# Value product on 64x64 tiles, one matmul per head; attention weights copied once; in-weight rows in their own order; tokens by groups; a new written opening

## The chip, the cores and the metric

The kernel runs on one core of one Trainium2 chip. The metric is the device time of one execution in microseconds. Before the change, three runs gave 1189.91 to 1191.05 us with a median of 1190.45 us. All durations below come from one further execution, taken with the hardware profiler.

Names of the engines: PE is TensorE (matmuls), PEld its weight loads, DVE is VectorE, ACT is ScalarE, POOL is GpSimd, SP is SyncE, which issues the DMAs here.

## The reference, cut to what matters

Chunked attention with a few memory keys, then two feed-forward layers. Four batches, 8 heads, 768 positions, head size 64; chunks of 32 queries see 8 memory keys, 16 positions to the left, their own 32 and 8 to the right, 64 keys in all.

```python
for c in range(nc):                       # 24 chunks of 32 queries, per batch and head
    k_full = np.concatenate([mem_k, k_ctx], axis=2)   # up to 64 keys
    v_full = np.concatenate([mem_v, v_ctx], axis=2)
    scores = scale * np.matmul(q_c, k_full.transpose(0, 1, 3, 2))
    a = np.exp(scores - np.max(scores, axis=-1, keepdims=True))
    a = a / (np.sum(a, axis=-1, keepdims=True) + 1e-09)
    out[:, :, c_start:c_end] = np.matmul(a, v_full)
x = out.transpose(0, 2, 1, 3).reshape(3072, 512)
h = x @ w_in;  x = (h * sigmoid(1.702 * h)) @ w_out              # 512 -> 2048 -> 512
g = x @ w_gate;  y = (silu(g) * (x @ w_val)) @ w_out2            # 512 -> 1536 -> 512
```

## The kernel before, in words

**Tiling.** The 3072 tokens are 6 blocks of 512 tokens; a block is 4 groups of 128 tokens, a group 4 chunks of 32. One group is one attention job over all 8 heads, so there are 24 groups. Each goes through: scores on TensorE (`scores_first` for the first eight groups, `scores` for the rest), maximum and subtraction on VectorE (`exponents`), exponential on ScalarE, sums and normalisation on VectorE (`st_sums`, `st_weigh`), a transposition of the weights on TensorE into PSUM (`turn`, L158), copies of the transposed weights into SBUF on ScalarE (`keep_e`, L167), the value product on TensorE (`values`, L174), a copy of its output into x (`keep_x`, L188), and a store of x (`store_x`, L193).

**The value product.** Head pair `a`, chunk `c`: the 128 rows of the transposed weights hold the 64 keys of the even head above the 64 keys of the odd head. `keep_e` writes them as a block diagonal (`ebd`, even head in the upper rows and one half of the columns, odd head in the lower rows and the other half); its other blocks are cleared once (`zero`). The product contracts over all 128 rows, with the 64 value columns as the loaded operand and 64 columns of `ebd` as the streamed one. The output of head pairs `a` and `a + 1` goes to the upper and the lower 64 partitions. So the rows of x stand in another order than the reference's, and the rows of the in-weights are brought into that order when they are loaded: two DMAs of 256 KB for each in-weight tile, each onto 64 partitions, in runs of 128 numbers of 8 bytes (`load_raw`, L281). Other weight tiles take one DMA of 512 KB (L276).

**Weights.** They arrive as 8-byte numbers and are turned into fp32 words by ScalarE and VectorE (`take_words`, `shift_words`, `join_words`), then split into a high and a low part (`split_hi` on ScalarE, `split_lo` on GpSimd). Matmuls take three passes over high and low parts.

**Feed-forward.** A unit is one column block of a layer, computed with seven half-size products (a Strassen scheme): `Tokens` makes the sums of quarters of x, `unit` (and the letters `qa` to `qg` of the opening) the products, L450; `down` accumulates the output products, L585. The first block's first units are plain products, `plain_up`, L546.

**What sets the order.** PE, ACT, DVE and POOL run in the order in which the program is written. For the first part that order is a table of step names, `OPENING`, in which SP's loads stand too: `ldq`, `ldk`, `ldv`, `ldw` load q, k, v and a weight tile, `sc` is a group's scores, `te` its transposition, `ec` the copies, `pv` the value product, `hi`, `xf`, `xl` the parts of x, `ua` and `ub` a plain product. The number behind a name is the group or the tile. Groups 0 to 11 are in the table. Groups 12 to 23 are worked off between the parts of later units by `attention`, `run` and `PLACES`. Behind the opening a scheduler places SP's DMAs.

Of the kernel before, what the change touches and what calls it, by code (L numbers as in the profile page):

```python
# [57 lines left out]
def tile_attention_moe_moe(  # L58
# [11 lines left out]
    def pool(name, bufs, space=None):  # L70
# [89 lines left out]

    def weights_at(g):
        return ebd[g % 2 if g < 2 * GRP else 0]

    def keep_e(g, ps, engs):
        for e, copy in enumerate(engs):
            r = slice(64 * e, 64 * e + 64)
            copy(weights_at(g)[r, :, :, e, :], ps[r].rearrange("p a (c q) -> p a c q", c=4))  # L167

    def values(g, ps, v):
        ps = ps.rearrange("p (a q) -> p a q", a=KC)  # L170
        for a in range(0, HP, 2):
            for c in range(4):
                for j in range(2):
                    nc.tensor.matmul(  # L174
                        ps[64 * j : 64 * j + 64, a : a + 2, CH * c : CH * c + CH],
                        v[:, a + j, c, :],
                        weights_at(g)[:, a + j, c].rearrange("p e q -> p (e q)"),
                        start=True,
                        stop=True,
                    )  # L180
        return ps

    def keep_x(g, ps):
        b, i = divmod(g, GRP)
        if b not in xf:
            xf[b] = xpool.tile([P, KC, BLK], F32, tag="xf", name="xf")
        dst = xf[b][:, :, i * P : i * P + P]
        nc.scalar.copy(dst, ps)  # L188
        xq[g] = dst

    def store_x(g):
        b, i = divmod(g, GRP)
        nc.sync.dma_start(out=xd[b][:, :, i * P : i * P + P], in_=xq[g])  # L193

# [18 lines left out]
    def st_et(g):  # L213
        keep_e(g, turn(bank("ps_t"), et.pop(g)), (nc.scalar.copy,) * 2)

# [174 lines left out]
    class Tokens:  # L390


        def __init__(self, src, engs, apart=False):
            n = BLK // 2
            self.apart = apart
            self.b11, self.b12 = src[:, 0:2, :n], src[:, 0:2, n:]
            self.b21, self.b22 = src[:, 2:4, :n], src[:, 2:4, n:]
            self.engs = engs
            self.ops = [None] * 7

        def sum(self, k):
# [40 lines left out]

# [395 lines left out]
    def tokens():  # L838
        if not tok:
            tok.append(Tokens(xf[1], [G, G, G, V, G, V, V, V, G, V, V], True))  # L840
        return tok[0]
# [78 lines left out]
    OPENING = """  # L920
        z0 tb0 z1 ldk0 ldq0 ldq1 ldw0 ldq2 ldk1 ldk2 ldk3 sc0 ldv0 ldq3 mx0 ldq4 ex0 ldw1 pr0 sm0 cs0 sc1 ldv1
        ra0 ct0 ldv2 rc0 wa0 sc2 mx1 z2 ldq5 wg0 ex1 ldq6 wal0 te0 sm1 ldq7 mx2 ra1 sc3 ldk4 ec0 rc1 wg1 ex2 sm2
        pr1 ldw2 te1 mx3 ra2 pv0 ldk5 ec1 rc2 cs1 ldk6 ex3 ct1 ldk7 pv1 hi0 wg2 sumA0 ldv3 wv0 sm3 wb0 xf0 wbl0
        te2 ra3 ldw3 hiA0 sumB0 rc3 sc4 wg3 ec2 te3 mx4 wvl0 hiB0 pv2 loA0 ldw4 pr2 ldw5 ex4 cs2 loB0 sc5 ldv4
        xf2 sm4 xf1 ct2 xl0 st0 ra4 hi2 rc4 wg4 wa1 ldw6 ec3 wal1 sc6 mx5 ldw7 hi1 xl2 mx6 pv3 ex5 te4 ldk8 xl1
        sm5 ex6 sc7 hi3 sm6 ldq8 pr3 xl3 ra6 ra5 ldv5 pr4 cs3 ec4 rc5 ua0 ct3 ldv6 mx7 ldq9 sumA1 wb1 ua1 wv1
        pr5 st1 rc6 ex7 wg5 sumB1 ub0 hiA1 wg6 st2 xf3 loA1 ub1 cs4 hiB1 sm7 th0 ct4 wvl1 te5 st3 ra7 th1 ua2
        loB1 ldw8 gt0 ec5 rc7 gt1 wbl1 ub2 gc0 wg7 pr6 rs0 ldw9 gc1 cs5 pv5 th2 rs1 pr7 gt2 sc8 wo0 ct5 gc2 wol0
        pv4 ldk9 xf5 rs2 wo1 mx8 te7 ldv7 xf4 wol1 ldq10 te6 ec7 st4 cs6 ua3 st5 ct6 ex8 cs7 pr8 dn0 sm8 wo2 ct7
        ra8 wol2 ub3 ec6 rc8 ldw10 wg8 wo3 pv6 cs8 th3 wol3 ct8 dn1 pr9 ldv8 gt3 ldw11 wa2 pv7 cs9 wal2 gc3 ct9  # L930
        xf6 sc9 xf7 ldv9 rs3 sumA2 tc0 st7 ts0 te8 ldq11 tc1 dm1 ldk10 ts2 ts1 ec8 mx9 st6 dn2 tl0 tc3 ev1 pr10
        pv8 tl3 tc2 sy1 sumB2 ex9 qa0 ts3 ldv10 tc5 dm0 tl1 cs10 cp0 sm9 tc4 qc0 tl5 tl2 ev0 qb0 cu0 ct10 sy0
        tc6 qe0 tl4 ab0 ra9 qd0 pr11 tl6 wv2 sc10 rc9 cm0 wvl2 wg9 xf8 qf0 ldk11 ac0 hiA2 te9 ad0 hiB2 loA2 qg0
        st8 mx10 ka0 ldq12 dn3 ma0 loB2 kb0 ex10 dm2 mb0 kc0 ldw12 sm10 mc0 dm3 md0 ldw13 ra10 ec9 rc10 sc11 kd0
        ev2 wg10 pv9 wo4 ldk12 ev3 wol4 te10 cs11 xf9 ldv11 ya0 mx11 ec10 st9 sy3 sy2 yb0 ct11 ex11 sm11 wo5
        pv10 pr12 wol5 ldw14 ra11 yc0 pr13 rc11 ldv12 wg11 xf10 cs12 te11 st10 ct12 yd0 ec11 cs13 ldw15 ct13 wa3
        pv11 wv3 sumA3 qa1 xf11 ldv13 st11 qb1 cp1 wvl3 hiA3 qc1 sumB3 pr14 ab1 qd1 cu1 qe1 wal3 cm1 hiB3 qf1
        ac1 loB3 qg1 ad1 pr15 cs14 ka1 qa2 cs15 loA3 ldw16 ma1 kb1 qb2 cp2 mb1 kc1 qc2 ab2 mc1 qd2 kd1 cu2 md1
        qe2 cm2 ct14 qf2 ya1 ac2 wo6 ldw17 ad2 wol6 ct15 ka2 qg2 kb2 wo7 ldw18 yb1 ma2 wol7 kc2 yc1
    """  # L940
# [58 lines left out]
    for n, (ph, b, ua, ub) in enumerate(seq):  # L999
# [6 lines left out]
        for u in range(ua, ub):  # L1006
# [101 lines left out]
```

## Time and profile before

| | |
|---|---|
| median of three runs | 1190.45 us |
| the profiled execution: its own time | 1190.33 us |
| the profiled execution: span from first to last instruction | 1188.6 us |
| mean granted TensorE clock over the span | 0.991 |
| busy: PE, PEld | 1151.3 us (97%), 1039.6 us (87%) |
| busy: DVE, ACT, POOL | 652.1 (55%), 568.1 (48%), 354.9 us (30%) |
| chain that ended last, by engine | PE 86%, DMA 5%, DVE 3%, ACT 2%, issue 2%, POOL 1% |
| moved by DMA | 131.47 MB in 62920 packets, 26208 of them under 2 KB |

The busy share of TensorE is a mean over stages with different limits, so it is read by stage. Busy time of PE is the union of its records, and a matmul's end is modelled, so records overlap: what a group of matmuls costs is read from the distance between starts rather than from the mean length of one record.

### The profile page before, as it was taken

What the parts mean: (1) busy time and instruction counts of PE and PEld (TensorE: products, weight loads), DVE (VectorE), ACT (ScalarE), POOL (GpSimd) and SP (SyncE); (2) the same over time, 40 slices, a digit from 0 to 9 for tenths busy, and PEclk for the clock granted to TensorE, in tenths of its full rate; (3) what the DMA queues carried; (4) which work ended last, traced back from release to release, by engine and by line L of the source; (5) the groups of instructions that cost most, each with busy time, mean ns of one, the idle gap of its engine ahead of it and who ended that gap; (6) DMA issues with size and microseconds to landing.
All of it is one profiled execution on the core that took longest, in us unless ns stands there. A gap on an engine that the chain in (4) does not pass through costs nothing.

```text
span 1188.6 us, 22301 instructions
## 1 busy us (share of the span) xinstructions
PE 1151.3 (97%) x8908; PEld 1039.6 (87%) x8908; DVE 652.1 (55%) x1117; ACT 568.1 (48%) x1185; POOL 354.9 (30%) x321
## 2 busy tenths in 40 slices
PE   4889999999999999999999999999999999999998
PEld 3778888888989999999988989999999999999997
DVE  5886756565765444443466564453556554453553
ACT  4866555455565454444455544343445544243342
POOL 4564221202454232321235433021345521021010
PEclk9889999999999999999999999999999999999999
DMA  9977354441454313322333321210225130320302
GB/s 304 296 253 231 110 157 120 130 140 63 137 166 118 106 66 114 131 74 62 106 116 107 106 99 36 72 71 1 89 89 178 36 103 5 107 92 15 107 25 83
DMA packets 62920, 131.47 MB, mean 111 GB/s; under 512 B 5728, under 2 KB 26208, under 8 KB 60512
## 3 DMA queue, kind: packets, MB, share of 16 engines
q1 hardware_dynamic: 62816, 130.05, 34.9%
q8 instruction: 70, 1.15, 0.4%
q14 instruction: 34, 0.28, 0.1%
HBM read 98.57 MB, written 31.46 MB: 109 GB/s over the span
## 4 chain that ended last, share of the span: by engine, by line
PE 86%; DMA 5%; DVE 3%; ACT 2%; issue 2%; POOL 1%; SPq 0%; DVEq 0%; ACTq 0%; POOLq 0%
PE y L585 35%; PE ps_a L450 27%; PE ps_c L450 12%; PE ps_b L450 9%; DMA raw<-in_wr 2%; PE ps_s L201 1%; PE ps_o L174 1%; DMA q<-in_qg 1%; DMA w<-in_kg 1%; DMA xd<-xf 1%; PE ps_t L158 1%; PE ps_v L174 1%; ACT ebd L167 0%; PE ps_u L546 0%; ACT g L551 0%
## 5 line engine op out<-in xcount | busy, mean ns | idle before, releaser
L450 PEld LDWEIGHTS ps_a<-b,w 128*128 128x128 f32 x2832 | 384.3, 189 | 39.6 <-DVE ps_a L502 4.2
L450 PE MATMUL ps_a<-b,w 128*128 128x256 f32 x2832 | 397.5, 283 | 5.7 <-DVE ps_a L502 2.1
L585 PE MATMUL y<-gs,w 128*128 128x512 f32 x1152 | 298.6, 395 | 0.6 <-DVE gs L565 0.5
L585 PE MATMUL y<-w,gs 128*128 128x512 f32 x864 | 247.7, 395 | 0.6 <-DVE gs L565 0.5
L585 PEld LDWEIGHTS y<-gs,w 128*128 128x128 f32 x1152 | 204.2, 189 | 36.2 <-DVE gs L565 1.4
L450 PE MATMUL ps_c<-b,w 128*128 128x256 f32 x1224 | 179.1, 282 | 0.0
L450 PEld LDWEIGHTS ps_c<-b,w 128*128 128x128 f32 x1224 | 167.1, 190 | 8.8
L585 PEld LDWEIGHTS y<-w,gs 128*128 128x128 f32 x864 | 144.2, 190 | 14.4 <-DVE gs L565 1.7
L258 POOL TENSOR_TENSOR w<-wf,w 128x512 fp32r<-128x512 f32 (+1 forms) x68 | 78.3, 1152 | 222.0 <-ACT w L255 221.9
L450 PE MATMUL ps_b<-b,w 128*128 128x256 f32 x900 | 135.5, 287 | 1.7 <-DVE ps_b L821 1.2
L450 PEld LDWEIGHTS ps_b<-b,w 128*128 128x128 f32 x900 | 120.4, 193 | 5.9 <-issue 1.7
L553 ACT ACTIVATE g<-ps_b 128x512 f32<-128x512 f32 x72 | 43.1, 598 | 166.1 <-DVE ps_b L508 166.1
L436 DVE TENSOR_TENSOR b<-xl,b 128x512 fp32r<-128x512 f32 x72 | 64.3, 893 | 80.4 <-ACT b L432 80.3
L502 DVE TENSOR_TENSOR ps_a<-m,ps_a 128x256 f32<-128x256 f32 x115 | 48.9, 426 | 104.0 <-PE ps_a L450 98.0
L492 ACT COPY u<-ps_a 128x256 f32<-128x256 f32 x115 | 43.0, 373 | 107.8 <-PE ps_a L450 107.6
L415 POOL TENSOR_TENSOR xl<-xl,t 128x512 f32<-128x512 f32 x18 | 23.3, 1296 | 231.3 <-DVE t L412 230.0
L565 DVE TENSOR_TENSOR gs<-ps_a,gs 128x512 fp32r<-128x512 f32 x118 | 80.8, 685 | 10.2 <-ACT gs L561 9.8
L487 DVE TENSOR_TENSOR ps_b<-p,ps_b 128x256 f32<-128x256 f32 x115 | 49.2, 427 | 61.3 <-PE ps_b L450 54.0
L561 ACT CAST gs<-ps_a 128x512 fp32r<-128x512 f32 x118 | 69.8, 592 | 22.5 <-DVE ps_a L531 15.6
L531 DVE TENSOR_TENSOR ps_a<-g,ps_a 128x512 f32<-128x512 f32 x72 | 50.0, 694 | 45.7 <-PE ps_a L450 45.2
L483 ACT COPY p<-ps_a 128x256 f32<-128x256 f32 x115 | 43.0, 374 | 60.3 <-PE ps_a L450 56.4
L508 DVE TENSOR_TENSOR ps_b<-u,ps_c 128x256 f32<-128x256 f32 x102 | 43.5, 426 | 50.1 <-PE ps_c L450 49.8
(123 smaller groups left out, 1190.6 us busy)
## 6 DMA issues: line engine op xcount, KB each, us to landing
raw<-in_wr SPq DMA_DIRECT2D x49, 512.0 KB, 3.4
xl<-yd SPq DMA_DIRECT2D x12, 1024.0 KB, 4.8
vm<-in_vg SPq DMA_DIRECT2D x22, 512.0 KB, 6.0
kbd<-in_kg SPq DMA_DIRECT2D x32, 256.0 KB, 4.2
raw<-in_wr SPq DMA_DIRECT2D x30, 256.0 KB, 5.3
yp<-o SPq DMA_DIRECT2D x24, 256.0 KB, 3.8
xl<-xd SPq DMA_DIRECT2D x6, 1024.0 KB, 4.8
base<-yp SPq DMA_DIRECT2D x24, 256.0 KB, 3.4
```

Source lines behind the costliest of these rows:

```text
L258: nc.gpsimd.tensor_sub(w[:, 1, o : o + n], f, w[:, 0, o : o + n].bitcast(F32))
L436: self.engs[k].tensor_sub(x[:, 1], self.source(k), x[:, 0].bitcast(F32))
L450: nc.tensor.matmul(ps, w[:, a, o + kc * P : o + kc * P + P], x[:, c, kc, :], start=(start and kc == 0 and (a, c) == PASSES[0]), stop=(kc = ...
L483: nc.scalar.copy(p1, ca[:, :n])
L487: add(cb[:, :n], p1, cb[:, :n])
L502: add(ca[:, n:], m, ca[:, :n])
L508: add(cb[:, n:], u2, cc)
L531: late[0] = [lambda: nc.vector.tensor_mul(ca, t, ca), lambda: gs.append(cast(ca))]
L553: nc.scalar.activation(t, c, AF.Silu)
L561: nc.scalar.copy(x[:, 0], g)
L565: nc.vector.tensor_sub(x[:, 1], g, x[:, 0].bitcast(F32))
L585: nc.tensor.matmul(y, lhs, rhs, start=(first and o == 0 and (a, c) == PASSES[0]), stop=(ends and o == len(gs) - 1 and (a, c) == passes[-1]),)
```

## The change

Four things are done together. The value product takes each head by itself, on 64 rows and 64 columns of the array: the even head on the upper rows and left columns, the odd head on the lower rows and right columns. So the transposed weights need no block diagonal: one copy brings all 128 partitions and 512 columns over, into two buffers in turn, and nothing is cleared. The rows of x now come in the reference's order, so every weight tile is loaded by one DMA. And x is kept by groups, [128, group, 4, 128] instead of [128, 4, 512], in SBUF and in DRAM, and read through views that bring it back. The table `OPENING` is written anew.

```diff
@@ names and tiles
-        [dram.tile([P, KC, BLK], F32, name=f"{n}{i}") for i in range(NBLK)] for n in ("xd", "yd", "yp", "zp")
+        [dram.tile([P, *shape], F32, name=f"{n}{i}") for i in range(NBLK)]
+        for n, shape in (("xd", (GRP, KC, P)), ("yd", (KC, BLK)), ("yp", (KC, BLK)), ("zp", (KC, BLK)))
-    ebd = [apool.tile([P, HP, 4, 2, CH], F32, name="ebd")]
+    ew = [apool.tile([P, HP, P], F32, name=f"ew{i}") for i in range(2)]
@@ copy and value product
-    def keep_e(g, ps, engs):
-        for e, copy in enumerate(engs):
-            r = slice(64 * e, 64 * e + 64)
-            copy(weights_at(g)[r, :, :, e, :], ps[r].rearrange("p a (c q) -> p a c q", c=4))
+    def keep_e(g, ps):
+        nc.scalar.copy(ew[g % 2], ps)
     def values(g, ps, v):
         ps = ps.rearrange("p (a q) -> p a q", a=KC)
-        for a in range(0, HP, 2):
+        for a in range(HP):
             for c in range(4):
-                for j in range(2):
-                    nc.tensor.matmul(
-                        ps[64 * j : 64 * j + 64, a : a + 2, CH * c : CH * c + CH],
-                        v[:, a + j, c, :],
-                        weights_at(g)[:, a + j, c].rearrange("p e q -> p (e q)"),
-                        start=True,
-                        stop=True,
-                    )
+                q = slice(CH * c, CH * c + CH)
+                for e in range(2):
+                    r = slice(64 * e, 64 * e + 64)
+                    nc.tensor.matmul(ps[r, a, q], v[r, a, c, :], ew[g % 2][r, a, q], start=True, stop=True)
@@ x by groups
-            xf[b] = xpool.tile([P, KC, BLK], F32, tag="xf", name="xf")
-        dst = xf[b][:, :, i * P : i * P + P]
+            xf[b] = xpool.tile([P, GRP, KC, P], F32, tag="xf", name="xf")
+        dst = xf[b][:, i]
-        nc.sync.dma_start(out=xd[b][:, :, i * P : i * P + P], in_=xq[g])
+        nc.sync.dma_start(out=xd[b][:, i], in_=xq[g])
@@ weight tiles
-            if k >= 2 * NF1 or k % 4 > 1:
-                nc.sync.dma_start(out=raws[-1], in_=wr[k])
-                continue
-            src = wr[k].rearrange("(e d) (b a n) -> a d b e n", e=2, b=2, a=2)
-            for a in range(2):
-                dst = raws[-1][64 * a : 64 * a + 64].rearrange("d (b e n) -> d b e n", b=2, e=2)
-                nc.sync.dma_start(out=dst, in_=src[a])
+            nc.sync.dma_start(out=raws[-1], in_=wr[k])
@@ views of x in Tokens
-            self.b11, self.b12 = src[:, 0:2, :n], src[:, 0:2, n:]
-            self.b21, self.b22 = src[:, 2:4, :n], src[:, 2:4, n:]
+            self.b11, self.b12 = src[:, 0:2, 0:2], src[:, 0:2, 2:4]
+            self.b21, self.b22 = src[:, 2:4, 0:2], src[:, 2:4, 2:4]
...
+    def by_group(t):
+        return t.rearrange("p k (g n) -> p k g n", n=P)
+    def from_groups(t):
+        return t.rearrange("p g k n -> p k g n")
@@ the opening
-        if n < 2:
-            for e in range(2):
-                (V, G)[n].memset(ebd[n][64 * e : 64 * e + 64, :, :, 1 - e, :], 0.0)
-        else:
-            off_diagonal(kbd, G)
+        off_diagonal(kbd, G)
-        z0 tb0 z1 ldk0 ldq0 ldq1 ldw0 ldq2 ldk1 ldk2 ldk3 sc0 ldv0 ldq3 mx0 ldq4 ex0 ldw1 pr0 sm0 cs0 sc1 ldv1
+        tb0 ldq0 ldk0 ldw0 ldk1 ldq1 ldq2 ldq3 ldw1 ldk2 sc0 ldk3 pr0 ldv0 mx0 ldq4 sc1 ldk4 cs0 ex0 ct0 ldk5
...
```

How the order of instructions changes is shown at three places.

TensorE in the stretch after the opening, around the value product of group 12, before (a row is line, operation, output and operands, shape and count; `ps_o` is the value product's bank, `ps_a` and `ps_b` the banks of a unit, `y` the bank of an output product, `vm` a tile of values):

```order
L450 MATMUL ps_b<-b,w 128x256 x6
L585 MATMUL y_1405<-gs,w 128x512 x6
L450 MATMUL ps_a<-b,w 128x256 x6
L174 MATMUL ps_o<-ebd,vm_117 64x2x32 x16
L450 MATMUL ps_b<-b,w 128x256 x6
```

and now:

```order
L442 MATMUL ps_b<-b,w 128x256 x6
L577 MATMUL y_1657<-gs,w 128x512 x6
L442 MATMUL ps_a<-b,w 128x256 x6
L172 MATMUL ps_o<-ew_119,vm_117 64x32 x32
L442 MATMUL ps_b<-b,w 128x256 x6
```

Nothing has moved there; the value product has 32 matmuls on 32 columns where it had 16 on 64.

TensorE in the opening, from the third value product to the first plain product (`ps_k` are scores, `ps_t` transpositions, `ps_v` value products, `ps_u` the plain product; `w` is a spare weight tile that holds keys, values or the block diagonal), before:

```order
L174 MATMUL ps_v<-ebd,w 64x2x32 x16
L706 MATMUL ps_k<-w,q 32x64 x32
L706 MATMUL ps_k<-w,qq 32x64 x32
L174 MATMUL ps_v<-w,vm_117 64x2x32 x16
L158 MATMUL ps_t<-ident,e 128x128 x4
L706 MATMUL ps_k<-w,qq 32x64 x32
L546 MATMUL ps_u<-xh,w 128x512 x6
```

and now:

```order
L172 MATMUL ps_v<-ew_119,w 64x32 x32
L159 MATMUL ps_t<-ident,e 128x128 x4
L693 MATMUL ps_k<-w,qq 32x64 x32
L159 MATMUL ps_t<-ident,e 128x128 x4
L172 MATMUL ps_v<-ew_120,vm_117 64x32 x32
L159 MATMUL ps_t<-ident,e 128x128 x4
L693 MATMUL ps_k<-w,qq 32x64 x32
L538 MATMUL ps_u<-xh,w 128x512 x8
```

The plain product still stands behind four value products and eight score products; two transpositions, of groups 3 and 5, now stand between the third and the fourth value product.

SP's queue from its first load, before (a count of 2 on an in-weight row is the two halves of one tile):

```order
L690 DMA kbd<-in_kg 128x1024
L672 DMA q<-in_qg 128x512 x2
L281 DMA raw<-in_wr 64x4x128 x2
L672 DMA qq<-in_qg 128x512
L690 DMA kbd<-in_kg 128x1024
L690 DMA w<-in_kg 128x1024 x2
L692 DMA vm_117<-in_vg 128x1024
```

and now:

```order
L663 DMA q<-in_qg 128x512
L677 DMA kbd<-in_kg 128x1024
L267 DMA raw<-in_wr 128x512
L677 DMA kbd<-in_kg 128x1024
L663 DMA q<-in_qg 128x512
L663 DMA qq<-in_qg 128x512 x2
L267 DMA raw<-in_wr 128x512
L677 DMA w<-in_kg 128x1024 x2
L679 DMA vm_117<-in_vg 128x1024
```

The second weight tile now stands ahead of the first tile of values, and each weight tile is one DMA.

## Rows read from the trace of the kernel before

**Rows 1.** Four stretches: bounds, length, busy PE, PEld, DVE, ACT, POOL, clock, DMA, GB/s.

```profile
0.00:41.30 41.30, 19.75 (x598) 16.16 (x599) 25.15 (x48) 21.47 (x47) 17.67 (x26) 0.83 1.01 308
41.30:131.50 90.20, 84.47 (x860) 71.78 (x859) 69.41 (x105) 60.94 (x121) 50.48 (x42) 0.96 0.72 216
131.50:300.00 168.50, 166.30 (x1607) 144.07 (x1600) 103.33 (x179) 87.59 (x181) 30.33 (x24) 1.00 0.45 130
300.00:1188.60 888.60, 880.81 (x5853) 807.61 (x5851) 454.22 (x786) 398.13 (x838) 256.38 (x230) 1.00 0.27 87
```

**Rows 2.** Waits of PE, 41 to 130 us: total us, times, longest.

```profile
PE ps_a L450 <- ACT p L816: 1.2, 1, 1.2
...
PE ps_b L450 <- DVE ps_b L821: 1.2, 1, 1.2
...
PE ps_v L174 <- ACT g L551: 0.7, 1, 0.7
PE ps_v L174 <- ACT ebd L167: 0.7, 1, 0.7
```

**Rows 3.** Waits of PE, 130 to 300 us.

```profile
PE ps_o L174 <- ACT ebd L167: 1.4, 3, 0.5
```

**Rows 4.** Timeline around one value product: start us, length us, engine, line, count.

```profile
144.73 1.15 PE L174 MATMUL ps_o<-ebd,vm 128*64 128x64 f32 x32
...
145.81 0.63 PE L450 MATMUL ps_b<-b,w 128*128 128x256 f32 x3
```

**Rows 5.** Timeline of PE's loads, 144.7 to 144.8 and 145.8 to 146 us.

```profile
144.73 0.20 PEld L174 LDWEIGHTS ps_o<-ebd,vm 128*64 128x64 f32 x4
...
145.81 0.30 PEld L450 LDWEIGHTS ps_b<-b,w 128*128 128x128 f32 x2
```

**Rows 6.** Groups by line and shape: count, busy us, mean ns, idle before.

```profile
L450 PEld LDWEIGHTS ps_a<-b,w 128*128 128x128 f32 x2832 | 384.3, 189 | 39.6 <-DVE ps_a L502 4.2 <-ACT p L483 2.2 <-ACT p L816 1.4
...
L167 ACT COPY ebd<-ps_t 64x512 f32<-64x512 f32 x40 | 23.1, 579 | 9.1 <-PE ps_t L158 8.4
...
L174 PE MATMUL ps_o<-ebd,vm 128*64 128x64 f32 x384 | 13.8, 225 | 1.4 <-ACT ebd L167 1.4
L201 PEld LDWEIGHTS ps_s<-kbd,q 128*32 128x32 f32 x512 | 13.6, 113 | 2.7 <-issue 2.1
...
L174 PEld LDWEIGHTS ps_o<-ebd,vm 128*64 128x64 f32 x384 | 12.2, 138 | 4.5 <-ACT ebd L167 2.7 <-issue 0.7 <-ACT r L146 0.4
...
L188 ACT COPY xf<-ps_o 128x512 f32<-128x512 f32 x12 | 7.1, 589 | 10.9 <-PE ps_o L174 10.9
...
L677 POOL MEMSET w<- 64x512 f32 x2 | 1.0, 520 | 0.1
L677 DVE MEMSET ebd<- 64x512 f32 x2 | 1.0, 485 | 1.1 <-PEq L1097 0.9
```

**Rows 7.** Timeline of PE in the opening.

```profile
36.90 1.97 PE L174 MATMUL ps_v<-w,vm 128*64 128x64 f32 x32 [1.28 <-ACT e L134]
...
41.34 0.83 PE L706 MATMUL ps_k<-w,qq 64*32 64x64 f32 x62 [1.19 <-issue]
42.10 1.66 PE L546 MATMUL ps_u<-xh,w 128*128 128x512 f32 x6
```

**Rows 8.** DMA issues, 0 to 41 us: count, KB each, median us to landing.

```profile
raw<-in_wr SPq DMA_DIRECT2D x6, 256.0 KB, 10.1
w<-in_wr SPq DMA_DIRECT2D x3, 512.0 KB, 11.3
...
w<-in_wr SPq DMA_DIRECT2D x2, 256.0 KB, 12.2
```

**Rows 9.** Groups by line and shape, two ScalarE copies of 128x256.

```profile
L255 ACT CAST w<-wf 128x256 fp32r<-128x256 f32 x20 | 8.1, 405 | 1.0 <-DVE wf L301 1.0
...
L725 ACT CAST xh<-ps_v 128x256 fp32r<-128x256 f32 x8 | 2.6, 377 | 0.8 <-PE ps_v L174 0.7
```

More of the change, by code (lines that the diff above doesn't have):

```diff
@@ L213, in st_et @@
     def st_et(g):
-        keep_e(g, turn(bank("ps_t"), et.pop(g)), (nc.scalar.copy,) * 2)
+        keep_e(g, turn(bank("ps_t"), et.pop(g)))
     def st_pv(g):
@@ L404, in sum @@
             if k == 0:
-                self.t3 = cpool.tile([P, 2, BLK // 2], F32, tag="t3", name="t3")
+                self.t3 = by_group(cpool.tile([P, 2, BLK // 2], F32, tag="t3", name="t3"))
                 eng.tensor_sub(self.t3, self.b22, self.b12)
@@ L410, in sum @@
             elif k == 2:
-                self.t2 = cpool.tile([P, 2, BLK // 2], F32, tag="t2", name="t2")
+                self.t2 = by_group(cpool.tile([P, 2, BLK // 2], F32, tag="t2", name="t2"))
                 eng.tensor_add(self.t2, self.t3, self.b11)
@@ L419, in place @@
                 return t
-            return opool.tile([P, BLK], F32, tag="o", name="t").rearrange("p (k n) -> p k n", k=2)
+            return opool.tile([P, BLK], F32, tag="o", name="t").rearrange("p (k g n) -> p k g n", k=2, g=2)
         def split(self, k):
@@ L431, in split_hi, with load_tokens @@
             self.ops[k] = bpool.tile([P, 2, 2, BLK // 2], F32R, tag="b", name="b")
-            nc.scalar.copy(self.ops[k][:, 0], self.source(k))
+            nc.scalar.copy(by_group(self.ops[k][:, 0]), self.source(k))
         def split_lo(self, k):
             x = self.ops[k]
-            self.engs[k].tensor_sub(x[:, 1], self.source(k), x[:, 0].bitcast(F32))
-    def load_tokens(src, engs):
-        t = xpool.tile([P, KC, BLK], F32, tag="xf", name="xl")
+            self.engs[k].tensor_sub(by_group(x[:, 1]), self.source(k), by_group(x[:, 0].bitcast(F32)))
+    def by_group(t):
+        return t.rearrange("p k (g n) -> p k g n", n=P)
+    def load_tokens(ph, src, engs):
+        shape = [P, GRP, KC, P] if ph == 1 else [P, KC, BLK]
+        t = xpool.tile(shape, F32, tag="xf", name="xl")
         nc.sync.dma_start(out=t, in_=src)
-        return Tokens(t, engs)
+        return Tokens(from_groups(t) if ph == 1 else by_group(t), engs)
+    def from_groups(t):
+        return t.rearrange("p g k n -> p k g n")
     PASSES = ((0, 0), (0, 1), (1, 0))
@@ L858, in tile_attention_moe_moe @@
         "te": turned,
-        "ec": lambda g: keep_e(g, at.pop(("e", g)), (nc.scalar.copy,) * 2),
+        "ec": lambda g: keep_e(g, at.pop(("e", g))),
         "pv": values_first,
@@ L926, in tile_attention_moe_moe @@
[L926 to L935, printed above, removed]
@@ new lines, in tile_attention_moe_moe @@
+        ldw2 sm0 wa0 z2 mx1 ra0 ldw3 pr1 rc0 sc2 ldq5 ex1 wal0 cs1 wg0 ldv1 ct1 te0 mx2 wb0 sumA0 sc3 ldv2 ec0
+        ldw4 wv0 sm1 hiA0 wvl0 ldk6 ra1 wbl0 pv0 ex2 mx3 sumB0 ldk7 rc1 ex3 sm2 sc4 loA0 ldv3 hi0 wg1 ra2 hiB0
+        rc2 ldq6 sm3 pr2 loB0 ldq7 wg2 ra3 pr3 rc3 ldw5 wg3 xf0 te1 xl0 mx4 st0 te2 ec1 sc5 cs2 ldq8 ec2 pv1 mx5
+        ex4 ldq9 pr4 sm4 ex5 pv2 ldv4 ct2 hi1 te3 sm5 xf2 ldv5 hi2 sc6 st2 cs3 ldw6 ra5 xl2 ec3 rc5 wg5 xf1 ldw7
+        ct3 ra4 wa1 st1 xl1 rc4 wb1 ldw8 wg4 wv1 pr5 ldw9 te5 mx6 pv3 wal1 te4 hi3 ldv6 sumA1 sc7 xf3 xl3 ldk8
@@ new lines, in tile_attention_moe_moe @@
+        ex6 ua0 sumB1 mx7 ec4 st3 ec5 wbl1 ub0 sm6 ex7 wvl1 sm7 ra6 hiB1 ua1 rc6 ra7 cs4 loB1 th0 rc7 cs5 pr6
+        ua2 wg7 pr7 ct4 pv5 hiA1 gt0 wo0 loA1 ub1 ct5 xf5 gc0 st5 wol0 wg6 ub2 wo1 rs0 th1 wol1 cs6 pv4 gt1 th2
+        gt2 gc1 ldv7 xf4 rs1 pr8 st4 ct6 sc8 gc2 cs7 wo2 dn0 rs2 ldq10 pr9 wol2 ldk9 ct7 tc0 te6 mx8 te7 ldw10
+        tl0 ec6 ua3 wo3 cs8 ex8 wol3 ct8 ub3 ec7 sm8 ldw11 wa2 cs9 pv7 ra8 wal2 th3 rc8 ct9 tc1 pv6 xf7 gt3 tl1
+        sc9 st7 wg8 gc3 ldv8 xf6 dn1 rs3 sumA2 ldq11 pr10 st6 ts0 ldk10 pr11 te8 ts1 ts2 dm1 ec8 ldv9 ts3 tc3
@@ new lines, in tile_attention_moe_moe @@
+        sumB2 mx9 dn2 wv2 tc2 tl3 tl2 ex9 pv8 tc5 sm9 tc4 qa0 wvl2 tl5 ldv10 ra9 tl4 rc9 qb0 cp0 cs10 tc6 qc0
+        hiA2 ab0 qd0 cs11 hiB2 loA2 wg9 sc10 cm0 ct11 cu0 loB2 qf0 ldk11 tl6 qe0 ad0 xf8 ldw12 dn3 ac0 ka0 st8
+        ct10 ldq12 te9 kb0 wo4 ldw13 qg0 ldw14 mx10 kc0 wol4 dm2 ma0 mb0 ex10 dm0 kd0 mc0 ev2 sm10 dm3 md0 sy2
+        ra10 ev0 rc10 sc11 ec9 wg10 sy0 wo5 ev3 te10 ldk12 pr12 wol5 pv9 mx11 ec10 sy3 qa1 pr13 ldv11 cs12 qb1
+        cp1 ct12 ex11 qc1 xf9 sm11 ldw15 qd1 st9 cu1 ab1 ra11 qe1 cm1 rc11 wa3 wg11 qf1 pr14 wal3 cs13 te11 ad1
@@ L940, in tile_attention_moe_moe @@
+        ya0 ec11 ct13 ka1 ac1 sumA3 pv11 wv3 kb1 pr15 ev1 qg1 kc1 sumB3 sy1 yb0 kd1 ma1 hiA3 mb1 wvl3 yc0 cs14
+        mc1 loA3 hiB3 md1 xf11 ct14 loB3 qa2 st11 yd0 cs15 cp2 ct15 wo6 ldw16 ldw17 qb2 wol6 wo7 ldw18 qd2 ab2
+        wol7 qc2 cm2 qf2 cu2 qe2 ad2 ya1 ka2 ac2 kb2 qg2 kc2 yb1 ma2 yc1 pv10 xf10 ldv12 st10 ldv13
     """
```

20 lines of the change are left out of this document (4 added, 16 removed).

## The prediction

> **What bounds the kernel now.** I read the windows first, cut at four places [rows 1]: the opening up to the first feed-forward product (41.3 us), the rest of the written opening (to 131.5), the stretch in which attention for the later blocks is spread between the units (to 300), and the remainder. The reader is to see that TensorE is busy 166.30 of 168.50 us in the third and 880.81 of 888.60 us in the fourth: there every microsecond added to TensorE is added to the kernel, and nothing taken from another engine gives more than what TensorE waits. In the first stretch it is the reverse: 19.75 of 41.30 us, with the DMA share at 1.01, so transfers and the chain behind them set the pace. The second lies between: 84.47 of 90.20 us, a gap of 5.73 us.
>
> Then the waits of TensorE [rows 2, 3]. In 41 to 130 us the larger ones go to a ScalarE copy (p, 1.2), a VectorE sum (1.2), the gate curve (0.7) and the copy of the turned weights (ebd, 0.7). In 130 to 300 us the largest is again that ebd copy, 1.4 us in three waits. Last, one value product in order of time [rows 4]: 32 records in 1.15 us, and the product behind it starts 1.08 us after the first of them.
>
> **The value product.** Before, a group has 16 matmuls, each 128 rows deep, 64 columns of values as weights, 64 columns of the block-diagonal tile streamed. Each leaves two records in the trace, so 32. The last lasts 0.225 us [rows 6], so the other starts are spread over 1.15 - 0.225 = 0.93 us: 0.029 us per record, or 0.058 us per pair, one record on each half of the array's columns. After, a group has 32 matmuls, so 64 records, again alternating between two places in the array (upper rows with left columns, lower rows with right). Each streams 32 columns, but each still loads 64 columns of values. So streaming per group is unchanged (32 pairs with half the columns, 32 x 0.029 = 0.93 us), and loading doubles.
>
> What a load costs is in the rows. At the start of the burst four loads of 64 columns (two per half) span 0.20 us with 0.138 for the last, so the second load of a half starts some 0.06 us behind its first; with 128 columns two loads span 0.30 with 0.189 for the last, so 0.11 us [rows 5, 6]. The mean load lasts 113, 138 and 189 ns for 32, 64 and 128 columns [rows 6]: 0.8 ns per further column, or 0.051 us for 64. Now the load of 0.05 to 0.06 us and the stream hide each other exactly, at 0.058 per pair. With 32 columns streamed nothing covers the load, and a pair still takes 0.058: 32 x 0.058 = 1.86 us, 0.93 us more per group.
>
> The Trainium skill says the same of a load ("TensorE: Matmul & The Clock Gate", section on LDWEIGHTS): its time goes with the columns and not with the rows, columns / 1.2 in ns. By that 64 columns take 53 ns, as an estimate, and halving the rows saves nothing; rows 5 and 6 agree (50 to 60 ns). A rule that counted rows would make the loads half as long and the change free.
>
> Bounds: no row shows a 64-column load behind a 32-column stream. From below, the stream alone: 0.93 us per group, no change. From above, the two places do not overlap: 64 x 0.058 = 3.7 us, 2.8 more. I take 1.86, since the load is the row itself, and since matmuls on halves of the rows do run side by side here: the scores on 64x32 tiles show 62 records in 0.83 us, 0.013 each [rows 7].
>
> **Where it counts.** Twelve groups fall in the third stretch: 12 x 0.93 = 11.2 us, all on the path. Eight fall behind the first feed-forward product: 8 x 0.93 = 7.4 us, in a stretch where TensorE has 5.73 us free. Four come before it; the last of them took 1.97 us [rows 7], at the lower of the clock's two levels (1.2 GHz; the stretch's mean is 0.83 [rows 1]).
>
> **The copy.** Two 64x512 copies become one 128x512, priced by the same shape from the same memory at 589 ns, against 2 x 579 [rows 6]: 0.57 us less ScalarE per group and a shorter path from turn to value product. In the third stretch that ends the three ebd waits: -1.4 us. Next late there is VectorE's normalised weights, which the turn waits for, hidden behind the other units' products. Between 41.3 and 131.5 us ScalarE has 8 x 0.57 = 4.6 us less to do, and TensorE's listed waits on it are 1.2 + 0.7 + 0.7 = 2.6 us [rows 2]: I take all of these, -2.6, and none of VectorE's waits. Bounds: 0 to -5.73. Leaving out the clearing of the block-diagonal tiles takes a microsecond each from VectorE and GpSimd [rows 6] while the first transfers are still on their way: nothing.
>
> **The transfers.** In-weight rows now land in one DMA of 512 KB. Under the opening's load a 256 KB half took 10.1 to 12.2 us and a whole one 11.3 [rows 8], and the halves come two by two, so the saving per load is somewhere between nothing and a few microseconds of a queue that is full. But the new order also spends it: ahead of the fourth value tile, the last that the first feed-forward product needs, the queue now carries 10.0 MB (six q, eight k, five weights, four v) where it carried 9.5 (eight q, eight k, three weights, four v). At 308 GB/s [rows 1] 0.5 MB is 1.7 us later; the earlier copy and whole rows give about that back, and the fourth product itself, if the clock is low there as now, takes 2 us more. I put the first stretch at 0, between -4 and +4. Stores of x in 2 KB instead of 512 B runs change nothing on the path.
>
> The views by groups turn 256-column runs into two of 128. The nearest rows, ScalarE on 128x256, take 377 ns with 128-column runs and 405 with one run [rows 9]: nothing, within a few ns per instruction, on engines that TensorE hides from 131.5 us on.
>
> **The sum**, on the profiled execution's 1190.33 us (span 1188.6 plus 1.7 around it; the median of the three runs is 1190.45): +11.2 + 7.4 - 1.4 - 2.6 + 0 = +14.6, or 1205 us.
>
> **Rivals.**
> 1. The load doesn't bind. If a 64-row load cost half, a pair would take about 0.029 us, TensorE's work would stay, and the 4.0 us of waits would be gain, perhaps 2 more in the opening: 1184 to 1187, faster. It decides when a pair takes under 0.058 x (0.93 + 4.0/20)/1.86 = 0.035 us. Against it: the loads of [rows 5]. 9%.
> 2. The two places run one after the other: 20 x 2.8 = 56 us less 4: 1242. For it, that both halves write one PSUM bank, where the scores of the opening put theirs into two; against it, that they write different partitions, as the two column halves do now at 0.029 per record. The Trainium skill has the rule ("TensorEngine Tiling (Array Packing)", "Restrictions and Gotchas"): different row tiles cannot access one bank at the same time. No row here shows row halves in one bank. 5%.
> 3. The new order pays more than I count: all 5.73 us of waits go, and the first product comes 4 us earlier: 11.2 + 7.4 - 1.4 - 5.7 - 4 = +7.5, 1198, down to 1193 if the low clock of the second stretch (mean 0.96 [rows 1], some 3.5 us) goes too. For it, DMA at full share with fewer, longer packets; against it, the 10.0 MB. 16%.
> 4. The order costs: longer products at the low clock push the first stretch back by 4 us and new waits take 4 more: 1213. 10%.
>
> My forecast has the remaining 60%, with 1199 to 1210 as its own range. The range over the cases is 1191 to 1213. A measurement of this kernel tells 0.2%, 2.4 us, from no change: faster 0.09, same 0.04, slower 0.87.
>
> **What would show it.** The value product's 64 records should take about 2.05 us in the steady stretch, the product behind it starting about 2.0 us after the first, with a tile's loads 0.055 us apart; ebd's waits gone; the steady stretch's TensorE time up by about 11 us. The prediction is wrong if a value product still takes 1.15 us, or if the opening ends more than 8 us earlier against the same work.

## The result, and the profile after

The changed kernel takes 1203.01 us (median of four runs, 1200.78 to 1204.43) against 1190.51 us for the kernel before on the same chip: the ratio over all their runs is 1.0109, with a 95% interval of 1.0093 to 1.0124 (the two medians divide to 1.0105). The forecast was 1205 us. Its profiled execution took 1203.29 us, of which the span is 1201.5, so it is compared below with the span of 1188.6 before: 12.9 us more.

The page of the changed kernel: span, busy time of the engines with their instructions, and the bytes moved.

```profile
span 1201.5 us, 23774 instructions
...
PE 1173.9 (98%) x9676; PEld 1063.0 (88%) x9676; DVE 654.0 (54%) x1115; ACT 553.4 (46%) x1161; POOL 355.4 (30%) x319
...
DMA packets 47310, 131.57 MB, mean 110 GB/s; under 512 B 5472, under 2 KB 5472, under 8 KB 44896
```

TensorE is busy 22.6 us longer (1151.3 before), ScalarE 14.7 us shorter, and the same bytes go in a quarter fewer packets (62920 before). The shorter ScalarE time and the fewer packets did not make the kernel shorter. Where the time goes is read by stretches. Fixed bounds would cut different work in the two kernels, so the stretches run from one piece of work to the same piece in the other kernel: from the start to the first plain product, from there to the scores of group 12, and on to the end of the last value product. In the columns of [rows 1], before:

```profile
0.00:42.10 42.10, 20.51 (x661) 16.82 (x661) 25.25 (x48) 22.26 (x48) 18.24 (x27) 0.84 1.01 310
42.10:130.57 88.47, 82.77 (x773) 70.30 (x767) 68.95 (x104) 59.78 (x119) 49.91 (x42) 0.96 0.73 217
130.57:281.34 150.77, 148.57 (x1514) 127.93 (x1513) 90.65 (x160) 75.38 (x156) 21.01 (x17) 1.00 0.47 135
```

and after:

```profile
0.00:43.56 43.56, 28.24 (x792) 24.64 (x792) 25.70 (x45) 20.54 (x47) 21.34 (x28) 0.73 0.96 360
43.56:133.56 90.00, 86.90 (x1024) 74.94 (x1019) 70.50 (x104) 54.30 (x109) 47.27 (x39) 1.00 0.58 184
133.56:293.84 160.28, 159.24 (x1898) 139.18 (x1897) 90.52 (x160) 67.85 (x144) 21.00 (x17) 1.00 0.46 128
```

The reader is to see three things. In the first stretch TensorE is busy 7.7 us longer and idle 6.3 us less (15.3 us where it was 21.6). In the second its idle time falls from 5.70 to 3.10 us, and its mean granted clock, 0.96 before because part of it ran at the lower of the two levels (1.2 GHz), reads 1.00. In the third it is busy 10.7 us longer and idle 1.04 us where it was 2.20.

TensorE's timeline of the changed kernel, first the opening, then the scores of group 12, one value product of the steady stretch, and the last value product ("issue" in brackets is a stop in which TensorE waited for nothing that the profile names):

```profile
16.82 2.06 PE L172 MATMUL ps_v<-ew,vm 64*64 64x32 f32 x64
...
21.70 0.90 PE L693 MATMUL ps_k<-w,q 64*32 64x64 f32 x41 [2.47 <-issue]
...
25.55 1.06 PE L172 MATMUL ps_v<-ew,vm 64*64 64x32 f32 x14
28.04 2.87 PE L172 MATMUL ps_v<-ew,vm 64*64 64x32 f32 x49 [1.43 <-issue]
...
30.74 3.70 PE L172 MATMUL ps_v<-ew,w 64*64 64x32 f32 x63
34.37 1.11 PE L159 MATMUL ps_t<-ident,e 128*128 128x128 f32 x4
...
37.85 3.63 PE L172 MATMUL ps_v<-ew,vm 64*64 64x32 f32 x64
...
43.56 0.78 PE L538 MATMUL ps_u<-xh,w 128*128 128x512 f32 x1
...
133.56 1.08 PE L193 MATMUL ps_s<-kbd,q 128*32 128x128 f32 x32
...
147.60 2.06 PE L172 MATMUL ps_o<-ew,vm 64*64 64x32 f32 x64
149.58 0.62 PE L442 MATMUL ps_b<-b,w 128*128 128x256 f32 x3
...
291.78 2.06 PE L172 MATMUL ps_o<-ew,vm 64*64 64x32 f32 x64
```

And the same work in the kernel before (its first plain product, at 42.10 us, stands in [rows 7]):

```profile
18.61 1.50 PE L174 MATMUL ps_v<-ebd,vm 128*64 128x64 f32 x32
...
21.93 1.15 PE L174 MATMUL ps_v<-w,vm 128*64 128x64 f32 x32 [1.81 <-ACT w L167]
...
29.65 1.98 PE L174 MATMUL ps_v<-ebd,w 128*64 128x64 f32 x32
...
130.57 1.08 PE L201 MATMUL ps_s<-kbd,q 128*32 128x128 f32 x32
...
280.19 1.15 PE L174 MATMUL ps_o<-ebd,vm 128*64 128x64 f32 x32 [0.45 <-ACT ebd L167]
```

| from | to | before | after | difference |
|---|---|---|---|---|
| start | first plain product | 42.10 | 43.56 | +1.5 |
| first plain product | scores of group 12 | 88.47 | 90.00 | +1.5 |
| scores of group 12 | end of the last value product | 150.77 | 160.28 | +9.5 |
| there | end of the span | 907.3 | 907.7 | +0.4 |

The waits of TensorE after, 41 to 130 us and then 130 to 300 us, in the columns of [rows 2, 3]:

```profile
PE y L577 <- DVE gs L557: 1.2, 1, 1.2
PE ps_b L442 <- DVE ps_b L808: 0.9, 1, 0.9
PE ps_v L172 <- ACT ew L163: 0.4, 1, 0.4
...
PE y L577 <- DVE gs L557: 0.9, 2, 0.7
```

Of ScalarE's waits that were listed before, 0.4 us for the copy is left (0.3 for another ScalarE result is new), and a wait for VectorE's gs stands in part of their place.

The copy and the value product by line and shape, as in [rows 6]:

```profile
L172 PEld LDWEIGHTS ps_o<-ew,vm 64*64 64x64 f32 x768 | 23.3, 135 | 3.0 <-ACT ew L163 1.1 <-issue 0.7 <-ACT r L147 0.4
...
L163 ACT COPY ew<-ps_t 128x512 f32<-128x512 f32 x24 | 13.9, 586 | 8.5 <-PE ps_t L159 8.4
```

A load of 64 columns on 64 rows lasts 135 ns where it lasted 138 on 128 rows: halving the rows saved nothing. The one copy lasts 586 ns; 589 was reckoned.

### The profile page after: what moved, and what is told of

It is laid out like the page before. It is cut to its first block, busy times and chain, and to the rows that moved or that the text cites. A ratio compares the mean times of both kernels' runs of the same rounds, so it can differ in the third digit from the quotient of the medians.

```text
span 1201.5 us, 23774 instructions
## 1 busy us (share of the span) xinstructions
PE 1173.9 (98%) x9676; PEld 1063.0 (88%) x9676; DVE 654.0 (54%) x1115; ACT 553.4 (46%) x1161; POOL 355.4 (30%) x319
## 4 chain that ended last, share of the span: by engine, by line
PE 90%; DVE 4%; DMA 2%; issue 2%; ACT 2%; POOL 0%; SPq 0%; DVEq 0%; ACTq 0%; POOLq 0%
PE y L577 36%; PE ps_a L442 27%; PE ps_c L442 12%; PE ps_b L442 9%; PE ps_v L172 2%; PE ps_o L172 2%; PE ps_s L193 1%; PE ps_t L159 1%; DMA xd<-xf 1%; DMA raw<-in_wr 1%; DVE wf L287 0%; DVE e L154 0%; PE ps_k L693 0%; DVE gs L557 0%; DVE wf L282 0%
## 5 line engine op out<-in xcount | busy, mean ns | idle before, releaser
L577 PEld LDWEIGHTS y<-w,gs 128*128 128x128 f32 x864 | 144.0, 190 | 14.7 <-DVE gs L557 2.0
```

The costliest lines, as they stand in the source:

```text
L577: nc.tensor.matmul(y, lhs, rhs, start=(first and o == 0 and (a, c) == PASSES[0]), stop=(ends and o == len(gs) - 1 and (a, c) == passes[-1]),)
```

## Experiments

The theory: a pair of matmuls, one on each place of the array, cannot follow the one before it faster than a place takes 64 new columns, 0.058 us, so 64 records take twice the time of 32. Its rivals: the stream binds; each record has a price of its own; the two row halves of one PSUM bank do not overlap. Beside it two questions were open: what whole weight tiles gave, and what the new order gave. All ratios are to the kernel before, run on the same chip.

**The stream doubled, the loads as they are.**

```diff
-  matmul(ps[r, a, q], v[r, a, c, :], ew[g % 2][r, a, q])
+  w = slice(min(CH*c, P - 2*CH), min(CH*c, P - 2*CH) + 2*CH)      # 64 columns
+  matmul(ps[r, a, w], v[r, a, c, :], ew[g % 2][r, a, w])
```

> The changed kernel, but each value matmul streams 64 columns of weights instead of 32 (a window twice as wide that overlaps the next chunk's, so part of x is overwritten with another chunk's product); loads, counts and places in the array are the same. If the load of 64 columns sets the pace (0.058 us per pair of records), the wider stream hides behind it as it did before the change: a value product stays at 2.05 us, the whole at 1203 us, within 2. If the stream sets the pace, a pair takes 0.116 us, a product 3.9 us, and the whole 20 x 1.86 = 37 us more, about 1240 us.

Measured: 1201.49 us (1200.98 to 1202.6), ratio 1.0094 (1.0078 to 1.011), beside 1.0109 for the change. The value product on the timeline:

```profile
145.48 2.08 PE L173 MATMUL ps_o<-ew,vm 64*64 64x64 f32 x64
```

It has twice the columns to stream and takes 2.08 us instead of 2.06. The stream is hidden behind the load, and its rival falls.

**Each load cut in two of 32 columns, on column strips of their own.**

```diff
-  matmul(ps[r, a, q], v[r, a, c, :], ew[g % 2][r, a, q])
+  for h in range(2):
+      o = slice(64*e + 32*h, 64*e + 32*h + 32)
+      matmul(ps[o, a, q], v[r, a, c, 32*h : 32*h + 32], ew[g % 2][r, a, q])
```

> The changed kernel, but each value matmul is split in two that load 32 value columns each, onto a column strip of their own; 64 matmuls and 128 records per group on four strips, everything computed. If the load sets the pace, a strip's record takes the longer of a 32-column load and a 32-column stream, about 0.03 us, so 32 records per strip take 0.96 us, a product 1.0 to 1.3 us instead of 2.05, and the whole falls by 20 x 0.8 to 0.95 = 16 to 19 us to 1184 to 1188 us, under the kernel before. If each record costs TensorE 0.029 us whatever its shape (what 32 records in 0.93 us and 64 in 1.86 would show as well), a product takes 128 x 0.029 = 3.7 us plus its tail and the whole 1240 us. If a stream has a least length of some 64 columns, a product stays at 2.05 us and the whole at 1203 us.

Measured: 1205.31 us (1203.06 to 1208.67), ratio 1.0124 (1.0104 to 1.0144). The time was missed by some 20 us, yet the product came out as expected. Its timeline, a product of the steady stretch last:

```profile
17.03 1.01 PE L174 MATMUL ps_v<-ew,vm 64*32 64x32 f32 x88
22.40 0.76 PE L174 MATMUL ps_v<-ew,vm 64*32 64x32 f32 x40 [4.36 <-issue]
...
157.03 1.29 PE L174 MATMUL ps_o<-ew,vm 64*32 64x32 f32 x128
```

Its waits of TensorE, 0 to 160 us:

```profile
PE ps_v L174 <- issue: 14.1, 5, 4.4
...
PE ps_t L159 <- issue: 3.9, 1, 3.9
```

In the steady stretch 128 records take 1.29 us against 64 in 2.06: no fixed price per record explains that, so this rival falls too, and the load theory stands. What the products gained, TensorE lost in stops without a wait that the profile names, 14.1 us of them in value products. The trace shows instruction transfers of 16 KB on the DMA engines, and TensorE starts again 1.3 to 1.5 us after one of them: blocks at 20.92, 33.64, 37.13 and 182.90 us, starts at 22.40, 35.09, 38.42 and 184.26. The same holds for all ten stops of more than 0.6 us in the first 200 us, and for both stops in the opening of the changed kernel (blocks at 20.39 and 26.64, starts at 21.70 and 28.04 us). That the instructions had run out is read from these pairs of times; no run took the transfers away.

**The same split where the queues are emptier**, in groups 12 to 23 alone (`if g >= 12`).

> The changed kernel with the two 32-column loads per matmul for groups 12 to 23 alone; the opening's products as the change has them. With the split everywhere a product took 1.29 us instead of 2.05, but TensorE stood still for 14 us inside products of the opening, without a wait that the profile names and each time until 1.3 to 1.5 us after a 16 KB block of instructions had landed. If those stops are the whole reason why that version was no faster, this one takes 12 x 0.77 = 9.2 us less than the change, and up to 3.4 more for stops in the later groups: 1194 to 1197 us. If the split costs something in the later groups as well (the clock, ScalarE), 1200 us or more.

Measured: 1195.7 us (1194.0 to 1197.96), ratio 1.005 (1.0033 to 1.0068): within the expectation, 7.3 us less than the change. Its product and its only waits for instructions from 135 to 300 us:

```profile
148.62 1.29 PE L175 MATMUL ps_o<-ew,vm 64*32 64x32 f32 x128
```

```profile
PE ps_o L175 <- issue: 2.5, 2, 1.5
```

Twelve products at 0.75 us less are 9.0, less 2.5 of stops: 6.5. So about 0.75 us of each of the twelve steady products is the load, and it can be had back.

**The kernel before with the same split**: 64 records for a group, as many as the change has, but in short loads.

```diff
+  for h in range(2):
-  matmul(ps[64*j : 64*j + 64, a : a + 2, ...], v[:, a + j, c, :], ...)
+      matmul(ps[64*j + 32*h : 64*j + 32*h + 32, a : a + 2, ...], v[:, a + j, c, 32*h : 32*h + 32], ...)
```

> The kernel before, with each value matmul split in two that load 32 value columns each onto a column strip of their own: 32 matmuls and 64 records per group, the number that the change has, but with 64 columns still streamed. If the load is what the change pays for, nothing is gained or lost on TensorE here, since the stream of 64 columns (0.055 us) covers either load: a product stays near 1.15 us and the whole at 1190 us, up to 3 more where the doubled instructions run out in the opening. If the number of matmuls is what costs, a product takes 2.05 us and the whole 1203 us or more.

Measured: 1195.95 us (1194.44 to 1197.0), ratio 1.005 (1.0034 to 1.0066). Timeline, and waits of TensorE from 0 to 135 us:

```profile
48.18 1.22 PE L547 MATMUL ps_u<-xh,w 128*128 128x512 f32 x2
...
149.72 1.10 PE L175 MATMUL ps_o<-ebd,vm 128*32 128x64 f32 x64
```

```profile
PE ps_k L707 <- issue: 8.3, 2, 5.8
...
PE ps_v L175 <- issue: 2.2, 2, 1.8
```

The product takes 1.10 us for twice the records: in the steady stretch they are free. But the opening ends at 48.18 us instead of 42.10. The stops for instructions there are 10.5 us, against 2.8 before in the same stretch. The expectation had 0 to 3 us for them; the opening grew by 6, and the whole time by 5.6.

**Two column halves on the same rows**: both matmuls of a pair read the upper 64 rows.

```diff
-  matmul(ps[r, a, q], v[r, a, c, :], ew[g % 2][r, a, q])
+  matmul(ps[r, a, q], v[0:64, a, c, :], ew[g % 2][0:64, a, q])
```

> The changed kernel with both matmuls of a pair on the upper 64 rows (the even head twice, the odd head left out), still on the left and the right columns in turn: same counts, loads and streams, but the two places now differ in columns alone. With most neighbours in one place a product took 2.47 us, little over the 2.05 of the change, so a record on one place seems to cost some 0.03 us and the two places to overlap hardly at all. If it is the two row halves that keep each other from overlapping, this one overlaps and a product falls to 1.1 to 1.3 us. If each place needs 0.055 us per load and both overlap already, or if a load costs 0.03 us wherever it goes, it stays at 2.05 us.

Measured, one run: 1202.73 us. The product:

```profile
146.48 2.06 PE L172 MATMUL ps_o<-ew,vm 64*64 64x32 f32 x64
```

2.06 us, as in the change. Two row halves that write different partitions of one bank overlap as two column halves do.

**Places that don't alternate.** In one kernel the four chunks of the even head come before the four of the odd one, for each head pair (loops a, e, c instead of a, c, e):

> The changed kernel with the value matmuls of one head pair in another order: four chunks of the even head, then four of the odd one, so that most neighbours use the same place in the array. If two records overlap only where neighbours use different places, most of a product runs one record at a time, 0.055 to 0.058 us each: up to 3.5 us per product instead of 1.84 and the whole up to 20 x 1.4 = 28 us more, 1220 to 1232 us. If the array takes records ahead of their turn, a product stays at 2.05 us and the whole at 1203 us.

In another all 16 matmuls of the even heads come first, then all 16 of the odd ones (loops e, a, c):

> The changed kernel with all 16 even heads' matmuls of a group first and then all 16 odd ones, so that the place changes once per product. If a place by itself needs 0.055 us per 64-column load, as the prediction read the first loads of a burst, and the change's order overlaps two places, a product takes 64 x 0.055 = 3.5 us plus its tail. If a record costs about 0.03 us on one place too, it takes 64 x 0.03 = 1.9 us plus its tail, as in the change, and the overlap of the two places is worth nothing.

Measured, one run each: 1208.15 and 1262.16 us. Their products, the first kernel's and then the other's:

```profile
148.08 2.47 PE L172 MATMUL ps_o<-ew,vm 64*64 64x32 f32 x64
```

```profile
176.40 3.71 PE L172 MATMUL ps_o<-ew,vm 64*64 64x32 f32 x64
```

With one place all the time a record takes 3.71/64 = 0.058 us: this is the second rival's price (3.7 us), and it is what the alternation saves. The kernel came out at 1262, not at that rival's 1242; more of its time runs at the lower clock (a mean of 0.967 over the span, 0.990 in the change).

With the place changing every four matmuls, 2.47 us was neither of the two values expected (3.5 or 2.05): most of the two places' work still overlaps around the changes. How far TensorE looks ahead was not measured.

**The old order**, in the changed kernel: the table `OPENING` of before without the two steps that clear tiles (`z0`, `z1`).

> The changed kernel with the opening's table of the kernel before (without the two clearing steps of the block diagonal, which have nothing left to clear). After the change the stretch from the first feed-forward product to the scores of group 12 grew by 1.5 us though eight value products cost 7.2 us more in it. If the new written order gave those 5.7 us back (fewer waits, no stretch at the low clock near 80 us), the old order loses them: 1206 to 1210 us. If they come from the shorter copy and the whole weight tiles, which stay here, it is within 2 us of 1203.

Measured: 1204.68 us (1204.47 to 1205.44), ratio 1.0121 (1.0105 to 1.0136), which overlaps the change's 1.0093 to 1.0124. Its first plain product:

```profile
44.95 1.65 PE L538 MATMUL ps_u<-xh,w 128*128 128x512 f32 x3
```

It starts 1.4 us later than with the new order; from there to the scores of group 12 it is 90.57 us, with the new order 90.00. The difference of the medians, 1.7 us, is less than the intervals tell apart, so whether the new order is worth anything stays open; it isn't worth the several microseconds of the third rival. Nor did it end the low clock that the kernel before has in the second stretch, between 78 and 84 us: here too the granted clock reads 1.00 from 50 us on.

**In-weights in halves**, in the changed kernel: the two DMAs of 256 KB for each in-weight tile, as before.

```diff
-  nc.sync.dma_start(out=raws[-1], in_=wr[k])
+  for a in range(2):                      # runs of 1 KB onto 64 partitions each
+      dst = raws[-1][64*a : 64*a + 64].rearrange("d (b e n) -> d b e n", b=2, e=2)
+      nc.sync.dma_start(out=dst, in_=src[a])
```

> The changed kernel with the in-weight tiles loaded as before, in two DMAs of 256 KB onto 64 partitions each in runs of 1 KB (this puts their rows into the order of the kernel before, so the first layer's products are other numbers). If the whole tiles are worth little, since the opening's order is paced by more than these loads, the time is 1203 to 1206 us. If the transfers pace the opening and 1 KB runs move at two thirds of the rate of the longer ones, 16 tiles cost 4 to 7 us: 1207 to 1210 us.

Measured: 1209.13 us (1206.76 to 1211.42), ratio 1.0157 (1.0137 to 1.0176): 6.1 us above the change. Its first plain product, 2.9 us later than with whole tiles:

```profile
46.41 0.80 PE L544 MATMUL ps_u<-xh,w 128*128 128x512 f32 x1
```

**Whole tiles in the kernel before**, and nothing else of the change: the rows of the in-weights are put in the order of its x in the layout in which they lie in DRAM, and each tile comes by one DMA.

```diff
+  wi = wi.reshape(NF1, 2, 64, 2, 2, P).transpose(0, 4, 2, 3, 1, 5).reshape(NF1, P, DM)
-  (two DMAs for each in-weight tile)
+  nc.sync.dma_start(out=raws[-1], in_=wr[k])
```

> The kernel before, with its block diagonal, its order of x and its opening, but with the in-weight rows laid out in DRAM in the order that its x needs, so that each in-weight tile is one DMA of 512 KB with 4 KB runs, as after the change. Loading the changed kernel's tiles in halves cost about 6 us. If that is the price of 1 KB runs in an opening paced by transfers, it is to be had here too: 1184 to 1188 us. If it depends on the new order, where the weights stand earlier in the queue, the time is 1189 to 1191 us.

Measured: 1183.14 us (1182.56 to 1184.2), ratio 0.9943 (0.993 to 0.9956). It beats both kernels, and lies just under the 1184 to 1188 expected. Its timeline and its DMA issues in the first 41 us (count, KB each, median us to landing):

```profile
36.89 1.22 PE L540 MATMUL ps_u<-xh,w 128*128 128x512 f32 x2
```

```profile
raw<-in_wr SPq DMA_DIRECT2D x4, 512.0 KB, 9.0
w<-in_wr SPq DMA_DIRECT2D x4, 512.0 KB, 10.0
```

The first plain product starts 5.2 us earlier than before, and a whole tile lands in 9 to 10 us where its halves took 10.1 and 12.2 [rows 8]. In these 41 us 14.39 MB arrive, against 12.59 MB before: not the latency of one load but the whole queue got faster. A half differs from a whole tile in two things, runs of 1 KB instead of 4 KB and 64 partitions instead of 128; no run tells apart which of them slows the queue.

## Why the prediction was right, and where it was wrong

The forecast of 1205 lies 2 us above the measured 1203, in its own range of 1199 to 1210, and its main mechanism, the load that binds, is the one that the runs show. That the sum came so close is in part luck: the second stretch was put 3.3 us too high and the first 1.5 us too low.

**The value product: right.** It said 64 records in about 2.05 us, the next product about 2.0 us after the first, and loads 0.055 us apart. Measured: 2.06 us and 1.98 us, and four loads in 0.19 us with 135 ns for the last, so again 0.055:

```profile
147.60 0.19 PEld L172 LDWEIGHTS ps_o<-ew,vm 64*64 64x64 f32 x4
```

The doubled stream, the 32-column loads and the single place bear out why.

**The steady stretch: right.** Said +11.2 - 1.4 = +9.8 us; measured +9.5. Twelve products at 1.98 - 1.08 = 0.90 are 10.8, and TensorE's idle time in the stretch fell by 1.2.

**The second stretch: the sum too high by 3.3.** Said +7.4 - 2.6 = +4.8; measured +1.5. The products cost 8 x 0.90 = 7.2. The waits are right in size, by luck in part: the idle time fell by 2.6, of which ScalarE's waits gave 2.1 and GpSimd's, which the step had not counted, 0.8, while VectorE's stayed at some 2.1. What the step left out is the clock. Before, TensorE ran at the lower level between 78 and 84 us:

```profile
78.42 1.65 PE L450 MATMUL ps_b<-b,w 128*128 128x256 f32 x6 [1.17 <-DVE ps_b L821]
...
84.02 1.07 PE L450 MATMUL ps_a<-b,w 128*128 128x256 f32 x6
```

The same work in the same order, in the kernel before with whole tiles, at the full clock:

```profile
74.16 0.98 PE L444 MATMUL ps_b<-b,w 128*128 128x256 f32 x6 [1.16 <-DVE ps_b L815]
...
77.25 0.96 PE L444 MATMUL ps_a<-b,w 128*128 128x256 f32 x6
```

From start to start that is 5.60 us against 3.09, so the lower level cost 2.5 us, and 7.2 - 2.6 - 2.5 = +2.1 (one transposition less stands in the stretch now, which is part of the 0.6 that is left). The prediction had seen the mean of 0.96 and given it to the third rival only. Why it went is open. It is gone too in the variants with the old order, with halves and with the doubled stream, and in the kernel before with whole tiles or with split loads; with every load of the change cut in two, some of it is still there (0.92 from 70 to 80 us, 0.91 from 80 to 90). With whole tiles TensorE is busy only 7.7 us of 70 to 80 and the clock still reads 1.00. (The clock's row alone is not enough: it reads 1.00 through the opening of the late split, where a product of 64 records takes 3.62 us. But in none of the variants without the low clock does a group of scores in the second stretch take the 1.94 us of the one at 80.00 us before.) So it is not shown to be a gain of this change's idea.

**The first stretch: right by two errors.** Said 0 between -4 and +4; measured +1.5. The step counted 2 us for the fourth value product and "about" 1.7 back from the earlier copy and whole rows. The rows show larger terms on both sides. The four value products up to the first plain product took 2.0, 5.2 (with 1.43 of stop), 3.6 and 3.6 us from their start to the next work, 14.4 in all, against about 1.5, 1.1, 1.9 and 1.9 before: 8 us more. The last three ran at the lower level (63 records in 3.70 us where the first product's 64 took 2.06), as the last two did before, and at that level the 0.9 us more of a product become 1.7. All four stand ahead of the first plain product on an engine that works in order. The step had put the first three at nothing, as it read the stretch as paced by transfers; in the changed kernel TensorE waits for no transfer after 13 us, and its own work counts from there on. (The 8 us less the stop of 1.43, and one transposition more, are the 7.7 us by which TensorE is busy longer.) Against that stand 6.5 us that came back. TensorE's waits for transfers up to the first plain product fell from 14.6 to 10.9 us, by 3.7, and the two waits for ScalarE that the lines of before show (1.81, and 1.28 in [rows 7]) are gone; the stops without a named wait grew from 2.8 to 3.9. Whole tiles alone move the first plain product by 5.2 us (7 us of the whole time) in the kernel before and by 2.9 (6.1) in the changed one; how the rest divides between the shorter copy and the new order is not shown. The whole rows are the other term that was mis-sized: the prediction compared the landing of one whole tile with that of one half [rows 8] and found next to nothing, where the question was how many bytes the full queue carries in the same time.

**Rivals.** The load that doesn't bind (1184 to 1187) is refuted by the product itself, and the two places one after the other (1242) too; its price is real, and the alternation avoids it. Of the third rival the clock came (2.5 us) and neither the earlier first product nor the last 3 us of waits; its lower end is 1198 - 3.5 = 1194.5 by its own terms, not 1193. Of the fourth the longer products at the low clock came, and of its 4 us of new waits 1.2 us for gs. The other parts, taken at nothing, show nothing: what lies behind the last value product differs by 0.4 us.

So the value products of all three stretches cost the change 8 + 7.2 + 10.8 = 26 us, and about half came back: 6.5 in the opening, in good part by the whole tiles, 3.8 of waits and 2.5 of clock. The kernel before with whole tiles has their gain without the cost. In the changed kernel itself splitting the loads gives 7.3 us back, as long as it is done behind the opening (1195.7 us).

## What to carry to other kernels

Cutting a matmul along the rows left the loading as it was. A narrow stream behind a wide load cost the load, so count columns loaded for each place of the array, not multiplications, and cut the load's columns rather than the stream's. When a change has several parts, price and try them one by one: here one gained and one lost, and the sum hid that. In a stage whose DMA queue is full, price a change of layout by the bytes that arrive in the same time, not by the latency of one transfer.

## What the runs showed that was not expected

- **Instructions arrive by the same DMA engines as the data.** Where matmuls are short, twice the records cost nothing in their own time (1.10 us for 64 against 1.15 for 32), but the opening came 6 us later, with TensorE stopped for up to 5.8 us at a time. The Trainium skill ("Runtime: NRT & Kernel Launch", section "Instruction fetch mechanics") has instructions refilled in blocks of 16 KiB, 256 instructions each, and calls the cost of crossing into a block mostly hidden. The size agrees with the 16 KB transfers here. The hiding does not hold where matmuls are this short: the stops are longest in the opening, where the DMA queue is full most of the time, but the kernel with every load cut in two also stops for 1.14 us up to 184.26 us, and there no data is on its way from 183 us on.
- **Row halves in one PSUM bank.** The Trainium skill's rule that the prediction weighed ("TensorEngine Tiling (Array Packing)", "Restrictions and Gotchas"), that different row tiles cannot access one bank at the same time, would have made the product 3.7 us long. The runs do not agree: 2.06 us with row halves and 2.06 with column halves on the same rows, each pair on different partitions of the bank.
- **A load of 64 columns takes as long on 64 rows as on 128** (135 and 138 ns a record, 0.058 us for each on one place), and split over two column strips the same columns go in 1.29 us instead of 2.06 for a whole value product.
